# Softmax sums into PSUM and an integer addition moved to VectorE, in an attention and two-MoE kernel on one Trainium2 core

## The chip, the cores and the metric

The kernel runs on one core of a Trainium2 chip. The core has a matrix engine (TensorE, PE in the rows; PEld is its weight load), three engines for elementwise work (VectorE or DVE, ScalarE or ACT, GpSimd or POOL), a queue engine that starts transfers (SyncE, SP), 16 DMA engines, an on-chip memory SBUF and a smaller one, PSUM, of eight banks (2 KB for each of 128 partitions), into which TensorE writes its results. Each engine works through its own instructions in order and waits by semaphores for the others. The metric is the device time of one execution in microseconds (us), lower is better.

## The reference

Three steps on 4608 tokens (batch 8, 576 positions); q, k, v are float32, the weights float64:

```
k_p, v_p = k, v averaged over groups of 8 positions        # (8, 8 heads, 72, 64)
scores = q @ k_p.T / sqrt(64);  scores -= max(scores)
attn = exp(scores);  attn /= sum(attn) + 1e-9;  x = attn @ v_p      # -> (4608, 512)
x = ((x @ w1) * (x @ w2)) @ w3 @ w_out                      # d_ff 1024
h = x @ w_in;  out = (h * sigmoid(1.702 h)) @ w_out2        # d_ff 2048
```

## The kernel before, in words

The weights come as float64, two 32-bit words for each number. `Conv` turns them into float32 on the chip, one 128x512 tile in each `step()`: ScalarE makes a float from the high word (L166) and a small integer from the low one (L168), VectorE shifts the first left by three bits (L169), and GpSimd adds the two as integers (L172), with both inputs and the output in SBUF. A later call splits the result for the matmuls: ScalarE copies the high part (L104), and VectorE or GpSimd, whichever the caller names, subtracts it to get the low part (L105). Every matmul by these parts is done as three (L114 to L116).

Forty conversions come first: 8 tiles of `w_out`, 16 of `w3` (turned by TensorE, L508), 8 of `w1`, 8 of `w2`; they run beside the first attention groups, the product w3 @ w_out and the first block of the first MoE. The other 32, of the second MoE's weights, come in its last two blocks (from about 620 us), where the shift reads PSUM instead of SBUF.

Attention works on 32 groups (one batch element, two heads). A group's steps are spread over "ticks": `g0` transposes k and q (L255, L256, VectorE), `g1` makes the scores in two PSUM banks (L278), takes their maxima (L283) and subtracts them into an SBUF tile (L285), `g2` takes the exponent (L294), `g3` does the rest of the softmax, all on VectorE: row sums (L300), the constant (L301), the reciprocal (L302), the multiplication (L303), then 32x32 transposes (L314). Sums and reciprocals stand in `nm`, a 128x10 tile in SBUF. `g4` splits the result (L368 to L372) and `g6` multiplies by v (L380 to L383) into the same two PSUM banks, and moves the outcome out (L390, L391).

The first MoE works on 9 blocks of 512 tokens; L638 and L641 form the product of its two halves. Blocks 0 to 6 carry the ticks of the remaining groups. The second MoE, from about 770 us, uses nothing that the change touches.

Loads are issued by SyncE in order. The order of the instructions on every queue is settled by the framework, which plans with a cost model of its own (`schedule_with_timeline_sim=True`) when the kernel is built.

Of the kernel before, what the change touches and what calls it, by code (L numbers as in the profile page):

```python
# [12 lines left out]
ALU = mybir.AluOpType  # L13
# [4 lines left out]
P = 128  # L18
T = 512
# [3 lines left out]
def pooled_attention_moe_moe2(  # L23
# [18 lines left out]
    nc = tc.nc  # L42
# [3 lines left out]
    SK = S // POOL  # L46
    DF1 = w1.shape[1]
    DF2 = w_in2.shape[1]
    w1, w2, w3, w_out, w_in2, w_out2 = (w.bitcast(U32) for w in (w1, w2, w3, w_out, w_in2, w_out2))
# [8 lines left out]
    TT = (S + P - 1) // P  # L58
# [36 lines left out]
    def give(*ts):  # L95
        for t in ts:
            if id(t) in held:
                free.append(held.pop(id(t))[1:])
# [19 lines left out]
    def col_tile(w, f):  # L118
        return w[:, 2 * f * P:2 * (f + 1) * P].rearrange("(c p) m -> p c m", p=P)

    def row_tile(w, f):
        return w[f * P:(f + 1) * P, :]

    def sl(i, n=P):
        return slice(i * n, (i + 1) * n)

    class Conv:
# [27 lines left out]
        def step(self):  # L155

            new = None
            if self.staged:
                t, turn, done = self.staged.pop(0)
                lo_w, hi_w = t[:, :, 0], t[:, :, 1]  # L160
                w = cv_p[0].tile([P, T], F32, name="cv", tag="cv", bufs=4)
                wu = w.bitcast(U32)

                e = self.ps[self.n % len(self.ps)] if self.ps else w
                self.n += 1
                nc.scalar.activation(  # L166
                    e, hi_w.bitcast(F32), AF.Prelu, scale=2.0 ** -112, alpha=-2.0 ** 32)
                nc.scalar.activation(lo_w.bitcast(I32), lo_w, AF.Copy, scale=2.0 ** -29)  # L168
                nc.vector.tensor_scalar(  # L169
                    out=wu, in0=e.bitcast(U32), scalar1=3, scalar2=None,  # L170
                    op0=ALU.logical_shift_left)
                nc.gpsimd.tensor_tensor(  # L172
                    out=w.bitcast(I32), in0=w.bitcast(I32), in1=lo_w.bitcast(I32), op=ALU.add)
                give(t)
                new = [w, turn, done]
            mid, old = self.line
            if mid and mid[1]:
                mid[0] = mid[1](mid[0])
            key = old[2](old[0]) if old else None
            self.line = [new, mid]  # L180
            self.load()
            return key
# [4 lines left out]
    conv = Conv()  # L187
# [3 lines left out]
    with pa_ctx:  # L191
# [7 lines left out]
            out=mask[:, 0], in_=mask[:, 0], compare_op=ALU.is_gt, fill=0.0,  # L199
            base=SK, pattern=[[0, D]], channel_multiplier=-1)  # L200
        nc.gpsimd.affine_select(
            out=mask[:, 1], in_=mask[:, 1], compare_op=ALU.is_ge, fill=0.0,
# [8 lines left out]
        for t in s_ts:  # L211
# [6 lines left out]
            out=ident, in_=ident, compare_op=ALU.is_equal, fill=0.0,  # L218
# [6 lines left out]
        g_q, g_k, g_v, g_s = {}, {}, {}, {}  # L225
# [38 lines left out]
        def banks_of(n):  # L264
            return acc[2:] if n < NPE and n % 2 else wk[2:]

        def s_of(n):
            return s_ts[n % 2 if n < NPE else 0]

        def g1(n):  # L270
            sc, s_t = banks_of(n), s_of(n)
            mov = kbd.rearrange("p a s -> p (a s)")
            nm = pa.tile([P, 2 * TT], F32, name="nm", tag="nm", bufs=2)
            g_s[n] = nm
            for half, tts in ((0, range(0, 3)), (1, range(3, TT))):
                w = len(tts) * KW
                for i, tt in enumerate(tts):
                    nc.tensor.matmul(  # L278
                        sc[half][:, i * KW:(i + 1) * KW], qT[:, sl(tt)], mov,
                        start=True, stop=True)  # L280
                ps = sc[half][:, :w].rearrange("p (a s) -> p a s", s=SK)
                m = nm[:, 2 * tts[0]:2 * tts[-1] + 2]
                nc.vector.tensor_reduce(out=m, in_=ps, op=ALU.max, axis=AX.X)  # L283
                na = 2 * len(tts)
                nc.vector.tensor_tensor(  # L285
                    out=s_t[:, tts[0]:tts[-1] + 1, :KW].rearrange("p t (a s) -> p t a s", s=SK),
                    in0=ps.rearrange("p (t a) s -> p t a s", a=2),
                    in1=m.rearrange("p (t a) -> p t a", a=2).unsqueeze(3).to_broadcast(
                        [P, na // 2, 2, SK]),
                    op=ALU.subtract)  # L290
# [3 lines left out]
            nc.scalar.activation(s_t[:, :, :KW], s_t[:, :, :KW], AF.Exp, scale=ESC)  # L294

        def g3(n):
            r, s_t = g_s.pop(n), s_of(n)
            pv = s_t[:, :, :KW].rearrange("p t (a s) -> p t a s", s=SK)
            rv = r.rearrange("p (t a) -> p t a", a=2)
            nc.vector.tensor_reduce(out=rv, in_=pv, op=ALU.add, axis=AX.X)  # L300
            nc.vector.tensor_scalar_add(r, r, 1e-9)  # L301
            nc.vector.reciprocal(out=r, in_=r)  # L302
            nc.vector.tensor_tensor(  # L303
                out=pv, in0=pv, in1=rv.unsqueeze(3).to_broadcast([P, TT, 2, SK]), op=ALU.mult)
            p0 = pa.tile([P, TT, P], F32, name="p0", tag="p0")
            p1 = pa.tile([32, TT, P], F32, name="p1", tag="p1")
            g_s[n] = (p0, p1)
            if n < NPE:
                return
            for r in range(5):  # L310
                for c in range(4):
                    nt = TT if 32 * (c + 1) <= S - (TT - 1) * P else TT - 1
                    dst = p0[32 * r:32 * r + 32] if r < 4 else p1[:32]
                    nc.vector.transpose(  # L314
                        out=dst[:, :nt, 32 * c:32 * c + 32],
                        in_=s_t[32 * c:32 * c + 32, :nt, 32 * r:32 * r + 32])
# [88 lines left out]
        def tick_first():  # L405

            t = tick_n[0]
            tick_n[0] += 1
            for n in range(NPE):
                if t == 2 * n + 6:  # L410
                    g6(n)
            for n in range(NPE):
                s = t - 2 * n
                if s == 0 and n == 0:
                    g0(0)
                elif s == 1:
                    g1(n)
                elif s == 2:
                    g2(n)
                    g0(n + 1)  # L420
                elif s == 3:
                    g3(n)
                elif s == 4:
                    g4(n)
                    g_va(n)
                elif s == 5:
                    g_vb(n)
            if t == 2 * NPE + 4:
                tick_n[0] = 4 * NPE
                give(s_sl)  # L430

        def tick():
            t = tick_n[0]
            if t < 4 * NPE:
                return tick_first()
            tick_n[0] += 1
            n, s = divmod(t, 4)
            if s == 0:
                if NPE <= n - 1 < NG:
                    g4(n - 1)  # L440
            elif s == 1:
                if n < NG:
                    g1(n)
            elif s == 2:
                if NPE <= n - 1 < NG:
                    g6(n - 1)
                if n < NG:
                    g2(n)
                    g_va(n)
                if n + 1 < NG:  # L450
                    g0(n + 1)
            elif n < NG:
                g3(n)
                g_vb(n)

        wo_s, wp_s, w1_s, w2_s = {}, {}, {}, {}
# [87 lines left out]
        def add_3(it, jh):  # L544
            conv.add(w3[sl(it), 2 * jh * T:2 * (jh + 1) * T], w3_turn(it, jh), w3_done(it, jh))

        for jh in range(2):
            for i in range(4):
                j = jh * 4 + i
                conv.add(row_tile(w_out, j), None,  # L550
                         conv.to(wo_s, j, nc.gpsimd if i % 2 else nc.vector, j,
                                 j if j < NA else None))
                if i < 2:
                    add_3(i, jh)
# [3 lines left out]
        for f in range(NF1):  # L558
            conv.add(col_tile(w1, f), None,
                     conv.to(w1_s, f, a=f - FA if 0 <= f - FA < NA else None))  # L560
            conv.add(col_tile(w2, f), None, conv.to(w2_s, f, nc.vector))

        conv.load()
        g_load(0)
# [107 lines left out]
    with tc.tile_pool(name="pb", bufs=1, reuse_waits="tile") as pb, \  # L672
# [238 lines left out]
        for pr in range(1, NPAIR + 1):  # L911
# [100 lines left out]
            m1, U, V, n = [], [], [], 0  # L1012
# [116 lines left out]
```

## Time and profile before

| | |
|---|---|
| median of 3 runs | 1483.03 us (1482.06 to 1484.38) |
| profiled execution: time | 1482.22 us |
| profiled execution: span | 1480.3 us |
| mean granted TensorE clock | 0.993 |
| busy share: TensorE, VectorE, ScalarE, GpSimd | 97%, 67%, 47%, 33% |

The span is the part of the time that the profile covers; 1.9 us lie around it. The shares are means over stages that differ: GpSimd, for one, has most of its work in the first half. A busy TensorE is not TensorE at its peak, since matmuls are pipelined.

### The profile page before, as it was taken

The page shows a single profiled execution, that of the slowest core. Times are in us where ns is not written, and L with a number is a line of the kernel's source. Part 1 is how long each engine was busy: PE and PEld are TensorE (multiplying, and loading weights), DVE is VectorE, ACT ScalarE, POOL GpSimd, SP SyncE. Part 2 cuts the span into 40 slices and gives each one's busy share as a digit, 9 for nine tenths or more (in the row PEclk, how much of TensorE's full clock was granted, in tenths as well). Part 3 has the DMA queues.
Part 4 walks back from the last instruction along what each step waited for, and adds up shares of the span by engine and source line. Part 5 has one row for each costly group of instructions (what it writes and reads, how often), then busy time and mean ns, then how long its engine had stood idle before and what let it go on. Part 6 is the DMA issues. An engine that isn't in the chain of part 4 may idle for free.

```text
span 1480.3 us, 19432 instructions
## 1 busy us (share of the span) xinstructions
PE 1437.6 (97%) x6536; PEld 1186.8 (80%) x6536; DVE 989.9 (67%) x1728; ACT 694.3 (47%) x1212; POOL 491.0 (33%) x589
## 2 busy tenths in 40 slices
PE   5978999999999999999999999999999999999998
PEld 3757888888888888888888887788788888888886
DVE  7889998878787877645536355693559354944554
ACT  6874444434343434366635335552455244634442
POOL 8787865555555555357743200000000000000000
PEclk8999999999999999999999999999999999999999
DMA  9992333323232321089879979867677766785665
GB/s 273 235 232 45 65 77 65 74 49 75 48 75 49 74 44 38 29 288 339 329 232 384 336 237 314 295 200 228 199 237 224 223 199 217 240 237 181 194 213 139
DMA packets 294435, 267.64 MB, mean 181 GB/s; under 512 B 201664, under 2 KB 226240, under 8 KB 294336
## 3 DMA queue, kind: packets, MB, share of 16 engines
q1 hardware_dynamic: 291648, 265.09, 59.8%
q10 hardware_dynamic: 2688, 1.31, 0.3%
q8 instruction: 52, 0.85, 0.2%
q14 instruction: 47, 0.39, 0.1%
HBM read 209.72 MB, written 56.62 MB: 180 GB/s over the span
## 4 chain that ended last, share of the span: by engine, by line
PE 85%; DVE 6%; DMA 4%; ACT 3%; issue 1%; SPq 0%; POOL 0%; DVEq 0%; ACTq 0%; POOLq 0%
PE bk L709 40%; PE wk L114 9%; PE wk L116 8%; PE wk L115 8%; PE acc L116 4%; PE acc L114 4%; PE acc L115 4%; PE wk L278 2%; DMA wud<-wt 2%; PE bk L115 1%; PE bk L116 1%; PE bk L114 1%; DVE s L105 1%; DVE cv L169 1%; DMA st<-wind 1%
## 5 line engine op out<-in xcount | busy, mean ns | idle before, releaser
L709 PE MATMUL bk<-mv,st 128*128 128x512 f32 x1152 | 271.5, 389 | 1.0 <-ACT mv L104 1.0
L709 PE MATMUL bk<-xM,st 128*128 128x512 f32 x1092 | 258.5, 390 | 3.2 <-ACT u L967 1.3
L709 PEld LDWEIGHTS bk<-mv,st 128*128 128x128 f32 x1152 | 216.1, 188 | 46.4 <-ACT mv L104 1.6
L709 PEld LDWEIGHTS bk<-xM,st 128*128 128x128 f32 x1092 | 204.5, 188 | 47.6 <-issue 2.5
L114 PE MATMUL wk<-s,s 128*128 128x512 f32 x576 | 227.9, 397 | 6.2 <-DVE a L641 3.6
L115 PE MATMUL wk<-s,s 128*128 128x512 f32 x576 | 225.4, 392 | 1.6 <-DVE s L391 1.5
L116 PE MATMUL wk<-s,s 128*128 128x512 f32 x576 | 225.3, 392 | 0.1
L314 DVE STREAM_TRANSPOSE p<-s_t 32x160 f32<-32x160 f32 (+1 forms) x560 | 178.5, 319 | 10.5
L115 PE MATMUL acc<-s,s 128*128 128x512 f32 x352 | 140.3, 399 | 1.2 <-POOL s L105 1.1
L116 PE MATMUL acc<-s,s 128*128 128x512 f32 x352 | 139.8, 397 | 1.6 <-DVE s L105 1.6
L114 PE MATMUL acc<-s,s 128*128 128x512 f32 x352 | 132.4, 402 | 7.4 <-DVE s L105 5.0
L114 PEld LDWEIGHTS wk<-s,s 128*128 128x128 f32 x576 | 108.7, 189 | 30.5 <-DVE a L641 4.7
L115 PEld LDWEIGHTS wk<-s,s 128*128 128x128 f32 x576 | 108.5, 188 | 24.0 <-DVE s L391 2.4
L116 PEld LDWEIGHTS wk<-s,s 128*128 128x128 f32 x576 | 108.5, 188 | 23.1 <-DVE s L105 0.5
L105 POOL TENSOR_TENSOR s<-a,s 128x512 fp32r<-128x512 f32 x56 | 73.4, 1310 | 155.1 <-ACT s L104 121.3
L105 DVE TENSOR_TENSOR mv<-g,mv 128x1024 fp32r<-128x1024 f32 x80 | 97.7, 1221 | 33.4 <-ACT mv L104 32.1
L104 ACT CAST mv<-g 128x1024 fp32r<-128x1024 f32 x80 | 84.3, 1053 | 72.5 <-PE bk L709 72.1
L172 POOL TENSOR_TENSOR cv<-cv,s 128x512 int32<-128x512 int32 x72 | 100.7, 1406 | 35.9 <-DVE cv L169 22.7
L114 PEld LDWEIGHTS acc<-s,s 128*128 128x128 f32 x352 | 67.2, 192 | 22.5 <-ACT s L104 4.6
L116 PEld LDWEIGHTS acc<-s,s 128*128 128x128 f32 x352 | 67.2, 191 | 15.7 <-DVE s L105 2.9
L115 PEld LDWEIGHTS acc<-s,s 128*128 128x128 f32 x352 | 67.3, 191 | 14.5 <-POOL s L105 2.3
L638 ACT COPY a<-wk 128x512 f32<-128x512 f32 x72 | 42.0, 583 | 68.4 <-PE wk L116 68.2
(188 smaller groups left out, 2341.8 us busy)
## 6 DMA issues: line engine op xcount, KB each, us to landing
st<-wud SPq DMA_DIRECT2D x96, 512.0 KB, 4.3
st<-wind SPq DMA_DIRECT2D x66, 512.0 KB, 4.7
st<-wind SPq DMA_DIRECT2D x76, 256.0 KB, 4.0
s<-in_moe_w_dram SPq DMA_DIRECT2D x32, 512.0 KB, 6.5
wind<-s SPq DMA_DIRECT2D x32, 512.0 KB, 5.4
s<-in_moe_w_out_dram SPq DMA_DIRECT2D x24, 512.0 KB, 6.6
kr<-in_k_dram SPq DMA_DIRECT2D x128, 72.0 KB, 2.5
qr<-in_q_dram SPq DMA_DIRECT2D x128, 72.0 KB, 2.5
```

Source lines behind the costliest of these rows:

```text
L104: nc.scalar.copy(dst[:, 0], src)
L105: lo_eng.tensor_tensor(out=dst[:, 1], in0=src, in1=f32(dst[:, 0]), op=ALU.subtract)
L114: nc.tensor.matmul(o, a[:, 0, a_sl], b[:, 0, b_sl], start=first, stop=False)
L115: nc.tensor.matmul(o, a[:, 0, a_sl], b[:, 1, b_sl], start=False, stop=False)
L116: nc.tensor.matmul(o, a[:, 1, a_sl], b[:, 0, b_sl], start=False, stop=last)
L169: nc.vector.tensor_scalar(out=wu, in0=e.bitcast(U32), scalar1=3, scalar2=None, op0=ALU.logical_shift_left)
L172: nc.gpsimd.tensor_tensor(out=w.bitcast(I32), in0=w.bitcast(I32), in1=lo_w.bitcast(I32), op=ALU.add)
L278: nc.tensor.matmul(sc[half][:, i * KW:(i + 1) * KW], qT[:, sl(tt)], mov, start=True, stop=True)
L314: nc.vector.transpose(out=dst[:, :nt, 32 * c:32 * c + 32], in_=s_t[32 * c:32 * c + 32, :nt, 32 * r:32 * r + 32])
L638: nc.scalar.copy(a, pa_)
L709: nc.tensor.matmul(o, w[:, x, m], b[:, y], start=first and n == 0, stop=last and n == 2, skip_group_check=True)
```

## The change

Three edits. In `g3` the 128x10 sums and reciprocals no longer stand in `nm` but in the last ten columns of the first of the group's two score banks in PSUM, which `g1` and `g6` leave unused (they take columns 0 to 431 and 0 to 287); the multiplication's two inputs change places, so that the reciprocals are the first. `nm` still takes the maxima. The integer addition L172 goes from GpSimd to VectorE, for all 72 tiles. The subtraction L105 of four of the eight `w_out` tiles and of all `w2` tiles goes from VectorE to GpSimd, so that it is there for all tiles of `w_out`, `w1` and `w2`.

```diff
@@ Conv.step
-                nc.gpsimd.tensor_tensor(
+                nc.vector.tensor_tensor(
                     out=w.bitcast(I32), in0=w.bitcast(I32), in1=lo_w.bitcast(I32), op=ALU.add)
@@ g1
-            g_s[n] = nm
@@ g3
-            r, s_t = g_s.pop(n), s_of(n)
+            s_t = s_of(n)
+            r = banks_of(n)[0][:, T - 2 * TT:]
...
             nc.vector.tensor_reduce(out=rv, in_=pv, op=ALU.add, axis=AX.X)
             nc.vector.tensor_scalar_add(r, r, 1e-9)
             nc.vector.reciprocal(out=r, in_=r)
             nc.vector.tensor_tensor(
-                out=pv, in0=pv, in1=rv.unsqueeze(3).to_broadcast([P, TT, 2, SK]), op=ALU.mult)
+                out=pv, in0=rv.unsqueeze(3).to_broadcast([P, TT, 2, SK]), in1=pv, op=ALU.mult)
@@ the list of conversions
-                         conv.to(wo_s, j, nc.gpsimd if i % 2 else nc.vector, j,
+                         conv.to(wo_s, j, nc.gpsimd, j,
...
-            conv.add(col_tile(w2, f), None, conv.to(w2_s, f, nc.vector))
+            conv.add(col_tile(w2, f), None, conv.to(w2_s, f))
```

## Rows read from the trace of the kernel before

**Rows 1.** Windows: stretch, length, busy (instructions) by engine, PEclk, DMA share, GB/s.

```profile
0.00:180.00 180.00, 148.59 (x686) 116.48 (x687) 152.74 (x262) 119.96 (x250) 144.13 (x171) 0.95 0.73 173
180.00:620.00 440.00, 439.45 (x2115) 370.68 (x2114) 359.75 (x887) 174.81 (x396) 232.44 (x332) 1.00 0.26 57
620.00:770.00 150.00, 149.97 (x664) 123.75 (x663) 74.72 (x108) 81.76 (x146) 90.84 (x72) 1.00 0.81 286
...
20.00:130.00 110.00, 91.25 (x434) 70.33 (x433) 96.27 (x143) 81.70 (x175) 91.13 (x101) 0.92 0.92 213
```

**Rows 2.** Waits of TensorE, 0 to 180 us: total us, times, longest.

```profile
PE wk L508 <- POOL cv L172: 10.6, 2, 9.2
PE acc L114 <- DVE s L105: 5.0, 3, 3.0
PE wk L114 <- DVE a L641: 3.6, 2, 1.9
...
PE acc L115 <- POOL s L105: 1.1, 2, 0.7
```

**Rows 3.** Groups of VectorE by shape, 0 to 180 us: count, busy us, mean ns.

```profile
L169 DVE TENSOR_SCALAR cv<-cv 128x512 uint32<-128x512 uint32 x40 | 30.8, 777 | 10.5 <-ACT cv L166 10.5
L105 DVE TENSOR_TENSOR s<-cv,s 128x512 fp32r<-128x512 f32 x12 | 14.4, 1198 | 1.5 <-ACT s L104 1.5
...
L303 DVE TENSOR_TENSOR s_t<-s_t,nm 128x720 f32<-128x720 f32 x6 | 10.3, 1714 | 0.1
L301 DVE TENSOR_SCALAR nm<-nm 128x10 f32<-128x10 f32 x8 | 9.5, 1182 | 0.1
...
L303 DVE TENSOR_TENSOR s<-s,nm 128x720 f32<-128x720 f32 x2 | 3.4, 1718 | 0.0
```

**Rows 4.** Single lines, whole span: ns min/median/max, first and last start.

```profile
L301 DVE TENSOR_SCALAR nm<-nm x32: 155/173/3399, 30.8 to 610.8; 128x10 f32<-128x10 f32 x32
...
L303 DVE TENSOR_TENSOR s_t<-s_t,nm x30: 895/899/4380, 33.9 to 611.2; 128x720 f32<-128x720 f32 x30
...
L169 DVE TENSOR_SCALAR cv<-wk x32: 675/681/692, 634.0 to 747.1; 128x512 uint32<-128x512 uint32 x32
...
L105 DVE TENSOR_TENSOR s<-wk,s x32: 656/691/693, 11.0 to 767.7; 128x512 fp32r<-128x512 f32 x32
```

**Rows 5.** Groups of GpSimd by shape, 0 to 180 us.

```profile
L172 POOL TENSOR_TENSOR cv<-cv,s 128x512 int32<-128x512 int32 x40 | 54.9, 1377 | 17.3 <-DVE cv L169 4.3 <-DMA s<-in_moe_w_dram 3.5 <-DMA kr<-in_k_dram 1.9
L105 POOL TENSOR_TENSOR s<-cv,s 128x512 fp32r<-128x512 f32 x12 | 15.5, 1295 | 3.0 <-ACT s L104 2.8
```

**Rows 6.** The ending chain within 0 to 155 us, shares by line.

```profile
by line: DVE s L105 9.2%; DVE cv L169 8.9%; DVE p L314 8.0%; DMA s<-in_moe_w_dram 6.6%; issue 6.4%; DVE nm L301 4.8%; DMA qr<-in_q_dram 4.8%; DVE s_t L303 4.5%; ACT cv L166 4.1%; ACT s L104 3.6%; ACT s L168 3.0%; PE wk L114 2.8%; DVE nm L30
```

**Rows 7.** Timeline near 83 us: start, us, instruction [idle before].

```profile
83.51 3.40 DVE L301 TENSOR_SCALAR nm<-nm 128x10 f32<-128x10 f32 x1
...
85.60 1.27 POOL L172 TENSOR_TENSOR cv<-cv,s 128x512 int32<-128x512 int32 x1
```

**Rows 8.** Timeline of the first two conversions.

```profile
5.51 0.43 DVE L169 TENSOR_SCALAR cv<-cv 128x512 uint32<-128x512 uint32 x1 [4.36 <-ACT cv L166]
...
6.66 0.65 ACT L168 ACTIVATE s<-s 128x512 int32<-128x512 uint32 x1
6.78 0.92 DVE L169 TENSOR_SCALAR cv<-cv 128x512 uint32<-128x512 uint32 x1 [0.84 <-ACT cv L166]
...
7.84 1.30 POOL L172 TENSOR_TENSOR cv<-cv,s 128x512 int32<-128x512 int32 x1 [0.42 <-DVE cv L169]
```

**Rows 9.** Timeline of one group's end in the steady state.

```profile
387.62 0.90 DVE L300 TENSOR_REDUCE nm<-s_t 128x10 f32<-128x720 f32 x1 [0.91 <-ACT s_t L294]
...
391.23 0.43 DVE L391 TENSOR_TENSOR s<-wk,s 128x256 fp32r<-128x256 f32 x1
...
399.37 1.42 POOL L372 TENSOR_TENSOR pt<-p,pt 32x576 fp32r<-32x576 f32 x1
...
407.99 0.29 PE L380 MATMUL wk<-ph,vm 128*128 128x288 f32 x1
```

## The prediction, made before any run of the changed kernel

> **What bounds the kernel now.** I read the busy time by stretch first [rows 1]. From 180 us to the end of the first MoE (770) TensorE has work nearly all the time: 439.45 us in 440, then 149.97 in 150. VectorE and GpSimd have room there. What the change does in those stretches is covered by TensorE, as long as no wait gets into TensorE's own queue. The first 180 us are the other kind: TensorE is busy 148.59 us, so 31.4 us are open, VectorE is busy 152.74 and GpSimd 144.13. The case is decided there.
>
> Next, who TensorE waits for in that stretch [rows 2]. The first wait, 9.2 of the 10.6 us put down to L172, is the start, before any weight is converted. Of the rest, VectorE's results (L105, L641) are named for 5.0 and 3.6 us and GpSimd's L105 for 1.1. So VectorE's queue makes TensorE late and GpSimd hardly does, directly.
>
> The row that names the lines of the ending chain within the first 155 us says the same [rows 6]: VectorE's L105, L169 and transposes lead it, and L301 and L303 stand in it with 4.8% and 4.5%, that is 7.4 and 7.0 us.
>
> Last, why L301 costs anything: it adds a constant to 10 columns. Its shortest execution takes 155 ns, the median is 173, but the longest 3399 [rows 4]; in the first 180 us its mean is 1182 over 8, and L303's is about 1.71 us against a median of 899 ns [rows 3, 4]. The timeline shows the long one beside GpSimd's L172 [rows 7]: L301 starts at 83.51 and is done at 86.91, as L172 (85.60, 1.27) ends. Other rows show which VectorE work is never stretched: L105 with one input in PSUM (wk) stays within 656 to 693 ns, and L169 reading wk within 675 to 692, although GpSimd works then too; the same L105 with both inputs in SBUF (cv) has a mean of 1198, and L169 in SBUF of 777 [rows 3, 4]. So an instruction wholly or partly on PSUM escapes GpSimd, and one with all its data in SBUF often waits for it.
>
> The Trainium skill says this as a rule ("SBUF — State Buffer", section "Who interferes with whom"): a VectorE instruction with two SBUF inputs contends with a GpSimd instruction that reads SBUF, and one with at most one SBUF input, outside the two-port modes, does not. The rows agree (1198 against 681 to 691 ns).
>
> **The change part by part.** All terms lie in the first 180 us.
>
> How much of a microsecond of VectorE work reaches the end: from below, the five VectorE entries shown on the chain add up to 35% of it [rows 6]; from above, VectorE is busy 96.27 of 110 us from 20 to 130, 88% [rows 1]. I take one half.
>
> 1. Sums and reciprocals in PSUM. L300, L301 and L302 then write the score bank; L303 has one SBUF input left. Excess today: L301 8 x (1.182 - 0.173) = 8.1 us; L303 10.3 + 3.4 - 8 x 0.90 = 6.5; together 14.6 on VectorE [rows 3, 4]. On the chain itself: 7.4 less four short executions (0.7), and 7.0 less three of 0.90, is 6.7 + 4.3 = 11.0 [rows 4, 6]. From below, half of 14.6 is 7.3. I take 11, since these pieces stand on the chain. What PSUM adds to four small instructions is not shown; L169 needs 0.68 from PSUM and 0.43 in SBUF at 512 columns [rows 4, 8], so at 10 columns next to nothing. Sum: -11.
>
> 2. L172 on VectorE. 32 of its 72 executions lie after 620, under a full TensorE [rows 1]: 0. The other 40 cost 0.68 us each, as L105 with the same 128x512 and no disturbance [rows 4]; no row shows an integer add with a stride on VectorE, so this is the nearest. 40 x 0.68 = 27.2, half is +13.6. Both inputs are in SBUF, so it may wait for GpSimd as L105 (cv) does: from below 0, from above 1.198 - 0.68 = 0.52 each. GpSimd's load in the stretch falls from 144.1 to 144.1 - 54.9 + 15.5 = 104.7 [rows 1, 5], and the most frequent thing to wait for, L172 itself, is gone. I take 0.25: 10 us, half is +5.
>    The same section of the Trainium skill speaks against this part: whichever of the two engines starts first keeps the port for its whole instruction. If each L172 met a whole GpSimd instruction of 1.38 us, that would be 55 us, half 28 in place of 5, and the sum +19. The row of L105 (cv), 0.52, says less.
>
> 3. L105 of four w_out and eight w2 tiles to GpSimd. VectorE loses 12 executions, 14.4 us [rows 3], half is -7.2. GpSimd takes 1295 ns for one [rows 5] against 1198 on VectorE, so the tile itself is ready no earlier; GpSimd has the room that L172 leaves.
>
> 4. L169 keeps its place, but the L172 it ran into is gone. Its excess is 30.8 - 40 x 0.43 = 13.6 us [rows 3, 8]. Between nothing and all of it I take half, 6.8, as GpSimd still has other work; half of that reaches the end: -3.4.
>
> 5. Start. The second conversion's low half is ready at 7.31 (6.66 + 0.65), its shift could be done at 7.21 (6.78 + 0.43). On GpSimd the add ends at 9.14, on VectorE it would at about 8.0 [rows 8]. Nothing else precedes the first matmul: -1.1.
>
> Sum: -11 + 13.6 + 5 - 7.2 - 3.4 - 1.1 = -4.1 us. The profiled execution has a span of 1480.3 us and a time of 1482.22, 1.9 around it; 1482.2 - 4.1 = 1478.1. The runs' median is 0.8 above the profiled one, so the same runs would show about 1479: 0.28% faster. A difference under 0.2% (3 us) can't be told from none here.
>
> The most there is to win is 31.4 - 9.2 = 22 us of open TensorE time. And the transfers are nearly at their limit: the DMA share from 20 to 130 is 0.92 [rows 1], so what VectorE gives back beyond a few microseconds would meet the weight loads as the next to be late.
>
> **The rivals.**
> - Nothing to measure, because the loads set the pace of the first 130 us (share 0.92), or because terms 1 and 2 cancel. For it: -11 and +18.6 are each larger than their sum. Time 1480 to 1486; about 1483.
> - Slower, by the queue of VectorE. If VectorE sets the stretch alone, every term counts in full: 27.2 + 40w - 14.4 - 6.8 - 14.6 - 1.1 = 40w - 9.7, where w is the wait of one L172. It decides at w = 0.24 us. With w = 0.52, as L105 (cv) has today, the sum is +11, 1494; with L169 unrelieved +18, 1501. For it: VectorE is at 88% and the change gives it more instructions than it takes. Against it: GpSimd's load falls by 27%.
> - Slower, by the bank. If the row sums must wait for other users of their PSUM bank, and not only for their own columns, then in the steady state L300 (387.62) has to come after the evacuation of the previous group's output (L391, done at 391.66): 4.0 us later. What hides it: GpSimd's L372 is done at 400.79 and TensorE takes the result at 407.99, 7.2 us later [rows 9]. Should the shift be longer than that in the 24 groups of that stretch, what is beyond stands in TensorE's queue; 0.3 us in each group is 7 us, 1490. The Trainium skill ("PSUM — Partial Sum Buffer", section "PSUM bank collisions raise a hardware error") says that two engines may not use one bank at the same time in the same partitions, so that a wait over the whole bank is likely; by the 7.2 us above it is hidden.
> - The PSUM form doesn't escape GpSimd. Then term 1 is 0 and the sum is +7, 1490. Rows 4 speak against it; small.
>
> The order on each queue comes from a planner whose costs the trace doesn't show. A new order can cost or give some microseconds anywhere in the first 180; this is in the range.
>
> **How the numbers follow.** Forecast, faster by about 4 us: 0.45. No measurable change: 0.25. Slower by VectorE's queue 0.18, by the bank 0.08, PSUM form useless 0.04: 0.30. Low end: no wait at L172 and L169's excess all gone, -11 + 13.6 - 7.2 - 6.8 - 1.1 = -12.5, so 1470. High end: VectorE alone with w = 0.52, +11, so 1494, which takes in the bank's 1490 and leaves out the worst.
>
> **What would show it.** L301 below 0.3 us and L303 near 0.90 in every execution: term 1 right. L172 on VectorE near 0.93 on average over the first 40: term 2; above 1.2 it is the second rival. VectorE busy about 154 us in the first 180 (152.7 + 27.2 + 10 - 14.4 - 6.8 - 14.6), GpSimd about 105, TensorE's open time there down from 31.4 to about 27. From 180 to 770 TensorE without gaps; a gap before L278 or L380 there would be the bank. I would be wrong if the open time before 180 grows although L301 and L303 are short: then the added L172 weighs more than the waits they removed.

## The result and the profile after

The changed kernel takes 1491.4 us (median of 6 runs, 1488.4 to 1494.2) where the kernel before takes 1483.7 beside it (1480.1 to 1485.1): ratio 1.0055, 95% interval 1.0040 to 1.0070. It is slower; the forecast had it 0.28% faster. The profiled execution took 1490.33 us, its span is 1488.6.

Windows of the changed kernel over the stretches of [rows 1], with the same columns:

```profile
0.00:180.00 180.00, 145.36 (x655) 114.63 (x656) 159.58 (x300) 120.16 (x250) 108.29 (x151) 0.92 0.71 175
180.00:620.00 440.00, 440.00 (x2125) 372.59 (x2124) 349.66 (x853) 172.98 (x392) 226.71 (x322) 1.00 0.26 56
620.00:770.00 150.00, 147.40 (x645) 121.37 (x644) 100.59 (x160) 81.50 (x146) 50.38 (x42) 0.99 0.80 286
```

Two stretches lost. In the first 180 us TensorE's open time grew from 31.4 to 34.6 us and its granted clock fell from 0.95 to 0.92. From 620 to 770, where nothing was open, 2.6 us are. From 180 to 620 there is no gap.

VectorE's groups by shape, first 180 us of the changed kernel (beside [rows 3]), then L301 and L303 over its whole span (beside [rows 4]):

```profile
L172 DVE CUSTOM_DVE_ANT_0 cv<-s,cv 128x1024 uint16<-128x1024 uint16 x40 | 33.7, 846 | 1.4
L169 DVE TENSOR_SCALAR cv<-cv 128x512 uint32<-128x512 uint32 x40 | 31.4, 790 | 6.8 <-ACT cv L166 6.6
```

```profile
L301 DVE TENSOR_SCALAR wk<-wk x30: 142/176/177, 30.7 to 621.5; 128x10 f32<-128x10 f32 x30
...
L303 DVE TENSOR_TENSOR s_t<-wk,s_t x30: 889/908/909, 32.6 to 622.0; 128x720 f32<-128x720 f32 x30
```

Nearly every duration came out as the prediction had it: L301 never above 0.18 us, L303 never above 0.91, L172 0.85 (0.93 was expected), VectorE busy 159.6 us (154) and GpSimd 108.3 (105). Only L169 got no relief, 790 ns against 777. And the time still went the other way. So the step that failed is not the price of L172, L301 or L303, but what a microsecond of VectorE is worth, and where.

### The profile page after: what moved, and what is told of

It reads as the page before. It is cut to its first block, busy times and chain, and to the rows that moved or that the text cites. A ratio compares the mean times of both kernels' runs of the same rounds, so it can differ in the third digit from the quotient of the medians.

```text
span 1488.6 us, 19393 instructions
## 1 busy us (share of the span) xinstructions
PE 1441.1 (97%) x6536; PEld 1192.4 (80%) x6536; DVE 1015.3 (68%) x1788; ACT 694.6 (47%) x1212; POOL 409.6 (28%) x529
## 4 chain that ended last, share of the span: by engine, by line
PE 84%; DMA 5%; DVE 4%; ACT 2%; issue 1%; POOL 1%; SPq 1%; DVEq 0%; ACTq 0%; POOLq 0%
PE bk L709 39%; PE wk L114 8%; PE wk L116 8%; PE wk L115 8%; PE acc L115 4%; PE acc L116 4%; PE acc L114 4%; PE wk L277 2%; DMA wud<-wt 2%; DMA s<-in_moe_w_dram 1%; PE bk L115 1%; PE bk L116 1%; PE bk L114 1%; DVE cv L172 1%; DMA st<-wind 1%
## 5 line engine op out<-in xcount | busy, mean ns | idle before, releaser
L709 PE MATMUL bk<-mv,st 128*128 128x512 f32 x1152 | 271.5, 389 | 0.4 <-DMA st<-wud 0.4
L709 PE MATMUL bk<-xM,st 128*128 128x512 f32 x1092 | 258.5, 390 | 2.4 <-DMA st<-wind 1.2
L709 PEld LDWEIGHTS bk<-mv,st 128*128 128x128 f32 x1152 | 216.1, 188 | 45.8 <-issue 1.0
L709 PEld LDWEIGHTS bk<-xM,st 128*128 128x128 f32 x1092 | 204.6, 188 | 46.6 <-issue 1.9
L105 DVE TENSOR_TENSOR mv<-g,mv 128x1024 fp32r<-128x1024 f32 x80 | 97.7, 1222 | 31.9 <-ACT mv L104 30.5
L104 ACT CAST mv<-g 128x1024 fp32r<-128x1024 f32 x80 | 84.3, 1054 | 70.4 <-PE bk L709 69.3
L638 ACT COPY a<-wk 128x512 f32<-128x512 f32 x72 | 42.2, 586 | 132.1 <-PE wk L116 113.1
L105 POOL TENSOR_TENSOR s<-a,s 128x512 fp32r<-128x512 f32 x56 | 73.2, 1308 | 101.8 <-ACT s L104 70.8
L369 POOL TENSOR_TENSOR ph<-p,ph 128x576 fp32r<-128x576 f32 x32 | 45.5, 1421 | 124.3 <-ACT ph L368 124.2
```

What stands on the lines that cost most here:

```text
L104: nc.scalar.copy(dst[:, 0], src)
L105: lo_eng.tensor_tensor(out=dst[:, 1], in0=src, in1=f32(dst[:, 0]), op=ALU.subtract)
L369: nc.gpsimd.tensor_tensor(out=ph[:, 1], in0=s0, in1=f32(ph[:, 0]), op=ALU.subtract)
L638: nc.scalar.copy(a, pa_)
L709: nc.tensor.matmul(o, w[:, x, m], b[:, y], start=first and n == 0, stop=last and n == 2, skip_group_check=True)
```

## Where the second loss is: the last 32 additions

TensorE's waits, 620 to 775 us, changed kernel; then its VectorE timeline there, TensorE's, and windows of 10 us:

```profile
PE wk L114 <- DVE s L105: 2.3, 1, 2.3
PE acc L114 <- ACT s L104: 0.3, 1, 0.3
```

```profile
737.45 2.88 DVE L172 CUSTOM_DVE_ANT_0 cv<-s,cv 128x1024 uint16<-128x1024 uint16 x2
...
746.45 1.76 DVE L172 CUSTOM_DVE_ANT_0 cv<-s,cv 128x1024 uint16<-128x1024 uint16 x1
748.13 0.68 DVE L105 TENSOR_TENSOR s<-wk,s 128x512 fp32r<-128x512 f32 x1
```

```profile
748.87 0.50 PE L114 MATMUL wk<-s,s 128*128 128x512 f32 x1 [2.26 <-DVE s L105]
749.20 0.39 PE L115 MATMUL wk<-s,s 128*128 128x512 f32 x1
749.43 0.40 PE L116 MATMUL wk<-s,s 128*128 128x512 f32 x1
...
750.81 0.63 PE L115 MATMUL wk<-s,s 128*128 128x512 f32 x1
751.23 0.63 PE L116 MATMUL wk<-s,s 128*128 128x512 f32 x1
```

```profile
730.00:740.00 10.00, 10.00 (x46) 8.29 (x45) 9.88 (x12) 7.71 (x14) 7.86 (x6) 1.00 0.79 264
740.00:750.00 10.00, 7.40 (x32) 5.50 (x31) 10.00 (x14) 5.15 (x10) 6.30 (x5) 1.00 0.70 277
750.00:760.00 10.00, 10.00 (x39) 8.06 (x38) 9.30 (x12) 4.65 (x8) 6.21 (x5) 0.83 0.65 225
```

VectorE is full from 730 to 750. L172 stands in front of L105 and lasts 1.76 us, and TensorE waits 2.26 us for that L105. After the gap the clock is granted at the lower of its two levels (1.2 against 2.4 GHz) for some 3 us: one matmul starts every 0.42 us (750.81 to 751.23) where just after the gap it was every 0.23 (749.20 to 749.43). The prediction's "32 of its 72 executions lie after 620, under a full TensorE" was read from a mean over 150 us (VectorE 74.72 busy, half). The kernel before, whose second MoE starts 9 us earlier, in the same two windows:

```profile
730.00:740.00 10.00, 10.00 (x46) 8.29 (x45) 6.65 (x10) 5.93 (x11) 10.00 (x8) 1.00 0.67 265
740.00:750.00 10.00, 10.00 (x46) 8.28 (x45) 7.19 (x9) 4.67 (x9) 10.00 (x9) 1.00 0.86 274
```

VectorE was free for 6.2 of these 20 us. The changed kernel's L172 takes 8.2 us of the 20.

## The experiments

Ratios are to the kernel before, run on the same chip, with 95% intervals. The last column is taken from the timeline of the profiled execution: when TensorE starts the second MoE (its first L709). It leaves out what happens later; the stretch from there to the end varies by several microseconds from profile to profile, with no work of it changed (707.3 to 717.5 us). Each entry is one execution: e1 and e8, whose orders differ by two instructions, lie 2.9 us apart.

| run | what differs from the kernel before | ratio | second MoE starts |
|---|---|---|---|
| before | | 1 | 770.58 |
| e1 | sums in PSUM | 0.9977 (0.9963 to 0.9992) | 765.66 |
| e2 | all 72 additions on VectorE | 1.0091 (1.0077 to 1.0105) | 778.55 |
| e3 | 12 subtractions on GpSimd | 1.0126 (1.0106 to 1.0146) | 785.30 |
| e4 | all three, last 32 additions on GpSimd | 1.0033 (1.0021 to 1.0045) | 775.59 |
| e5 | sums, subtractions | 1.0048 (1.0031 to 1.0065) | 779.15 |
| e6 | sums, first 40 additions | 1.0055 (1.0040 to 1.0071) | 775.35 |
| e7 | sums, last 32 additions | 1.0000 (0.9982 to 1.0017) | 767.76 |
| e8 | sums, first 2 additions | 0.9975 (0.9963 to 0.9988) | 768.54 |
| changed | all three | 1.0055 (1.0040 to 1.0070) | 779.64 |
| e10 | sums; first 40 shifts left out | 0.9975 (0.9951 to 1.0000) | 768.41 |
| e11 | sums, subtractions; shifts left out | 1.0026 (1.0016 to 1.0036) | 773.18 |
| e12 | all three; shifts left out | 1.0043 (1.0027 to 1.0059) | 775.61 |
| e13 | sums; L301 left out | 1.0021 (1.0010 to 1.0032) | 775.16 |
| e14 | sums; L301 twice | 1.0011 (1.0000 to 1.0023) | 771.90 |
| e15 | all three; L301 left out | 1.0080 (1.0064 to 1.0097) | 779.00 |
| e16 | all three; L301 twice | 1.0081 (1.0067 to 1.0095) | 778.47 |
| e17 | L300 in two parts | 1.0052 (1.0036 to 1.0068) | 775.70 |

### The parts alone

The theories at this point. A: the loss comes from L172 on VectorE, in the first stage and in the last 32, and the sums in PSUM gain. B: the sums' bank makes someone wait. C: only the planner's new order, within 5 us either way.

The edits are those of the diff ahead, each by itself; e4 is the whole change but for the last 32 additions:

```diff
@@ e4, Conv.step
-                nc.vector.tensor_tensor(
+                (nc.gpsimd if self.ps else nc.vector).tensor_tensor(
```

> Only the sums and reciprocals go to PSUM. Theory A (the loss comes from L172 on VectorE, the softmax part gives back waits): 4 to 8 us faster than before, 1476 to 1480, L301 under 0.2 us. Theory B (the bank makes other users wait): 3 us or more slower, 1487 or above, with gaps before L278 or L380 between 180 and 620. Theory C (any edit makes a new planned order, and the order alone moves the time): anywhere within 5 us of before.

> Only L172 goes to VectorE, all 72. Theory A: slower than the full change, since the waits of L301 and L303 stay and VectorE keeps the twelve subtractions: 1492 to 1500, with gaps of TensorE before 180 and about 745. Theory B: no slower than before, 1481 to 1486. Theory C: within 5 us of before.

> Only the twelve subtractions go to GpSimd. Theory A: VectorE is relieved by 14 us before 180 while GpSimd, at 144 of 180 us, gets 16 more: 0 to 4 us faster, 1480 to 1484. Theory B: as before, 1484. Theory C: within 5 us of before.

> The full change, but the last 32 integer additions (from 620 us on) stay on GpSimd. Theory A: the 2.6 us of open TensorE time near 745 and the slow matmuls behind it go, so 4 to 5 us less than the full change: 1486 to 1488. A rival A2 (all of the loss arises before 180): as the full change, 1490 to 1492. Theory B: as the full change.

e1 gains, as expected of it, 0.23%. But VectorE's busy time in the first 180 us fell by 5.3 us only (152.74 to 147.46), where L301 and L303 had 14.6 us of excess to lose. The same groups in e1:

```profile
L169 DVE TENSOR_SCALAR cv<-cv 128x512 uint32<-128x512 uint32 x40 | 36.3, 917 | 9.5 <-ACT cv L166 9.0
L105 DVE TENSOR_TENSOR s<-cv,s 128x512 fp32r<-128x512 f32 x12 | 16.1, 1343 | 0.7 <-ACT s L104 0.7
```

L169 went from 777 to 917 ns and L105 (cv) from 1198 to 1343 [rows 3]: 5.5 and 1.7 us of the freed time. In this order part of the wait for GpSimd moved to the instructions that still have all their data in SBUF. From 180 to 620 TensorE is busy 438.85 of 440 us in e1, 0.60 less than before [rows 1]: theory B finds no wait worth the name there.

e2 and e4 came out as theory A had them (1496.9 and 1487.6 us): the additions alone lose 0.91%, and taking the last 32 back to GpSimd wins part of the loss.

e3 was the surprise: moving the subtractions, which had looked like the safest gain, costs 1.26%. Its VectorE timeline near the end of the conversions:

```profile
128.54 7.49 DVE L301 TENSOR_SCALAR nm<-nm 128x10 f32<-128x10 f32 x1
136.07 0.22 DVE L302 RECIPROCAL nm<-nm 128x10 f32<-128x10 f32 x1
136.32 0.91 DVE L303 TENSOR_TENSOR s_t<-s_t,nm 128x720 f32<-128x720 f32 x1
137.33 6.64 DVE L314 STREAM_TRANSPOSE p<-s_t 32x160 f32<-32x160 f32 x20
144.00 0.69 DVE L641 TENSOR_TENSOR a<-wk,a 128x512 f32<-128x512 f32 x1
```

Ten columns take 7.49 us, beside a row of GpSimd instructions without a pause, and TensorE waits 8.9 us for the L641 at the end of this list. L301 is done at 136.03, in the first pause of GpSimd's row (136.00 to 136.08):

```profile
134.72 1.28 POOL L105 TENSOR_TENSOR s<-cv,s 128x512 fp32r<-128x512 f32 x1
136.08 0.31 POOL L342 TENSOR_TENSOR vt<-vtf,vt 32x64 fp32r<-32x64 f32 x1
```

I took that for the cause of e3's loss; e5 was to show it.

### The parts in pairs

> The sums and reciprocals in PSUM and the twelve subtractions on GpSimd; every L172 stays on GpSimd. Theory A (the subtractions alone lost time because L301, with its ten columns in SBUF, was kept waiting 7.5 us by a row of GpSimd instructions): with L301 on PSUM that wait can't occur, L301 stays below 0.3 us, VectorE loses 14 us of its own work in the first 180 us against the softmax part alone, and the time is 1475 to 1482 us, at or below the 1479.2 of the softmax part alone. Rival C (GpSimd's longer queue, 12 x 1.3 us more with all 40 L172, is what lost the time): 1490 us or more, with TensorE waiting for GpSimd's L105 or L172.

> The sums and reciprocals in PSUM and the first 40 integer additions on VectorE; the twelve subtractions stay on VectorE and the last 32 additions on GpSimd. Theory A (VectorE's queue in the first 180 us decides): VectorE is busy about 147 + 40 x 0.85 - 7 = 174 us at most there, 167 at least, more than the 159 of the version with the subtractions moved, and the time is 1488 to 1494 us. Rival C (the moved subtractions cost, not the additions): below 1484 us.

> The sums and reciprocals in PSUM and only the last 32 integer additions on VectorE. Theory A: about 4 us over the softmax part alone, 1482 to 1485 us, with the first 180 us as there (VectorE about 147 us, TensorE about 150.5) and TensorE's gap of 2 to 3 us near 745 us, put down to VectorE's L105. Theory C (a new order of the planner everywhere): the first 180 us differ by over 1 us of TensorE's time, and there is no gap near 745.

> The sums and reciprocals in PSUM and only the first two integer additions on VectorE. If the start's gain reaches the end (as the fifth term of the prediction had it): the first matmul at about 8.0 us instead of 9.1, and 1478 us, 1.1 below the softmax part alone. If a load or VectorE's queue takes it back: first matmul at 8.0 and 1479 to 1480 us.

e5 took that theory down. L301 is short there and VectorE is busy 130.7 us, 17 fewer than in e1, yet the kernel is 0.7% slower than e1. Its longest waits of TensorE between 20 and 60 us, and VectorE's timeline ahead of the first:

```profile
PE wk L351 <- DVE s_t L303: 4.5, 1, 4.5
PE wk L277 <- DVE qT L256: 4.0, 1, 4.0
```

```profile
27.20 2.56 DVE L169 TENSOR_SCALAR cv<-cv 128x512 uint32<-128x512 uint32 x1
...
30.49 1.53 DVE L169 TENSOR_SCALAR cv<-cv 128x512 uint32<-128x512 uint32 x1
...
32.28 1.44 DVE L169 TENSOR_SCALAR cv<-cv 128x512 uint32<-128x512 uint32 x1
33.65 0.89 DVE L303 TENSOR_TENSOR s_t<-wk,s_t 128x720 f32<-128x720 f32 x1
```

Now L169 is the one that waits, ahead of L303. The time is also in the range of e5's rival C (1490.7 us), the longer queue of GpSimd. TensorE's waits put down to GpSimd's L105 in the first 180 us, in e3 and in e5 (1.1 us in e1):

```profile
PE acc L115 <- POOL s L105: 4.1, 3, 1.8
PE acc L115 <- POOL s L105: 3.6, 3, 1.8
```

That is 2.5 to 3.0 us more than in e1, a part of these losses at most.

e6 takes 1491.9 us, in the range of theory A, but VectorE is busy 158.8 us and not 167 to 174: L169 falls to 620 ns there. So the time agrees and the load that was to explain it does not.

e7 gives the price of the last 32 additions a second time. From 119 to 631 us its L638 start within 0.1 us of those of e1. Then the gap comes, again 2.3 us and again put down to L105, and the ratio is 0.0023 above e1's. The pair e4 and the changed kernel gives 0.0022; their L638 starts lie 0.4 us apart from 185 to 641 us. Either is about 3.3 us. The intervals are wide for such a difference, but the gap is in both traces and in neither of the partners. The other versions agree: TensorE waits for VectorE's L105 between 620 and 775 us in all that have the last 32 additions on VectorE (1.6 us in e2, 2.3 in e12, 2.5 in e15, 0.5 in e16, where 1.9 more are put down to L104), and in none that leaves them on GpSimd.

The lower clock does not follow each time. In e7's trace it stays at 1.00 behind the gap, and the second MoE starts 2.1 us after that of e1; in the changed kernel's it fell, and the start is 4.1 us after that of e4:

```profile
730.00:740.00 10.00, 7.41 (x32) 5.50 (x31) 10.00 (x14) 5.41 (x10) 6.31 (x5) 1.00 0.71 281
740.00:750.00 10.00, 10.00 (x46) 8.15 (x45) 9.20 (x13) 4.24 (x8) 6.48 (x5) 1.00 0.63 214
```

e8 shows that a gain at the start does not come through: the first matmul is at 7.96 us instead of 8.81 in e1, with the same order on every queue but for the two additions, and neither the ratio nor the start of the second MoE is better. From 119 us on its L638 start 3.1 us later than those of e1. e7's first matmul, at 9.50 us, is 0.7 us later than e1's, and that is lost as well.

### What VectorE's time is worth

If VectorE's queue sets the pace, then less of it must help, whatever the reason for its load. The first forty shifts were left out of three versions:

```diff
@@ Conv.step
+                if self.ps:
-                nc.vector.tensor_scalar(
-                    out=wu, in0=e.bitcast(U32), scalar1=3, scalar2=None,
-                    op0=ALU.logical_shift_left)
+                    nc.vector.tensor_scalar(
+                        out=wu, in0=e.bitcast(U32), scalar1=3, scalar2=None,
+                        op0=ALU.logical_shift_left)
```

> The sums and reciprocals in PSUM; the first forty shifts L169 are left out (the weights come out wrong). VectorE loses 36 us in the first 180. If VectorE's queue sets the stretch by one half (the factor of the prediction): 18 us faster than the softmax part alone, about 1462 us, no less than 1458 (TensorE's open time there is 29.5 us, 8 of it the start). If the loads set it: 1474 to 1479 us.

> The sums and reciprocals in PSUM, the twelve subtractions on GpSimd, and the first forty shifts L169 left out. Theory A, mended (the subtractions on GpSimd cost 11 us because L169, in SBUF, waits for GpSimd's now unbroken row, and L303 stands behind it): without L169 the difference is gone, within 4 us of the version without shifts that keeps the subtractions on VectorE. Rival C (GpSimd's own queue is late): 8 us or more above that version.

> The changed kernel with the first forty shifts L169 left out. VectorE loses 31 us in the first 180. Theory A (after the change VectorE's queue sets the stretch): 15 us or more faster than the changed kernel, 1476 us or less. Rival (the loads, which lead the changed kernel's chain of waits, set it): 1486 us or more.

VectorE lost 31.7, 35.8 and 25.6 us of busy time in the first 180 us (147.46 to 115.78, 130.69 to 94.86, 159.58 to 133.95). The ratios fell by 0.0002, 0.0022 and 0.0012: 0.3, 3.3 and 1.8 us. That is 0.01 to 0.09 us for one of VectorE, where the prediction took one half. The intervals are as wide as these differences, and by the starts of the second MoE it is -0.09 to 0.17; one half would have been 13 to 18 us. My mended theory for e5 and the theory of VectorE's queue for the changed kernel fall with it: e11 is still 0.5% above e10, and e12, with 13.5 us less work on VectorE than e1, is 0.66% above e1 (0.22 of it the last 32 additions). Rival C's time for e11 (8 us or more above e10) is met by 8.3 us between the medians; but TensorE's waits put down to GpSimd's L105 are 1.8 us there, and its open time is no longer than e10's (29.3 and 30.0 us). What e11 loses by stays open. The line that names the ending chain within the first 155 us, e1 and then e10 (behind L169 the line numbers are one higher in e10):

```profile
by line: DVE cv L169 7.7%; DVE p L314 7.7%; DVE s L105 7.4%; PE acc L114 6.8%; PE acc L115 5.9%; PE acc L116 5.7%; issue 5.4%; DMA s<-in_moe_w_dram 4.4%; DMA qr<-in_q_dram 4.2%; SPq L229 4.1%; DMA kr<-in_k_dram 3.5%; PE wk L114 2.9%; PE wk 
```

```profile
by line: SPq L230 21.6%; DMA s<-in_moe_w_dram 18.6%; DVE s L105 6.7%; PE wk L116 4.3%; PE wk L114 4.2%; DVE p L315 4.1%; issue 3.9%; PE wk L115 3.8%; PE acc L114 3.2%; DMA kr<-in_k_dram 3.0%; PE acc L116 2.8%; PE acc L115 2.8%; SPq L151 2.7
```

Take VectorE's L169 out of the chain, and the loads (SyncE's issues and the weights' transfers) stand there with 40%. Two chains of nearly the same length side by side would look like this, and the one that the profile names is only the one that ended last. No run changes the loads, so that they set the pace is not shown.

### The same work in another order

What was left was the order of the queues, which the planner makes anew with each edit. L301 is 0.17 us of work and changes nothing in the result (it adds 1e-9 to a sum of at least 1). To leave it out or to do it twice gives the versions other orders for next to no work: in the traces, TensorE's instructions in e13 and e14 differ in their order from those of e1 by about as much as those of the changed kernel do.

```diff
@@ g3, e13 and e15
-            nc.vector.tensor_scalar_add(r, r, 1e-9)
@@ g3, e14 and e16
-            nc.vector.tensor_scalar_add(r, r, 1e-9)
+            nc.vector.tensor_scalar_add(r, r, 1e-9); nc.vector.tensor_scalar_add(r, r, 1e-9)
@@ g3, e17 (kernel before)
-            nc.vector.tensor_reduce(out=rv, in_=pv, op=ALU.add, axis=AX.X)
+            nc.vector.tensor_reduce(out=rv[:, :3], in_=pv[:, :3], op=ALU.add, axis=AX.X)
+            nc.vector.tensor_reduce(out=rv[:, 3:], in_=pv[:, 3:], op=ALU.add, axis=AX.X)
```

> The sums and reciprocals in PSUM, and L301 (0.17 us on ten columns, 32 times, 5 us of VectorE's 988) left out: it adds 1e-9 to a sum that is at least 1. The work is the same, but the planner makes another order, as far from that of the softmax part alone as the changed kernel's is. Theory D (the engines that do the work decide): 1477 to 1483 us, as the softmax part alone. Theory O (the order decides): anywhere in 1475 to 1492, and of the four runs of this kind at least one softmax version is above 1486 or one changed kernel below 1484.

> The sums and reciprocals in PSUM, and L301 done twice. Theory D: 1478 to 1484 us. Theory O: anywhere in 1475 to 1492.

> The changed kernel with L301 left out. Theory D: 1488 to 1494 us, as the changed kernel. Theory O: anywhere in 1475 to 1495.

> The changed kernel with L301 done twice. Theory D: 1489 to 1495 us. Theory O: anywhere in 1475 to 1495.

> The kernel before, with L300's sums taken in two instructions (three and two of its five tiles), about 0.1 us of VectorE more for each of 32 groups: the same work in another order. Theory D (the engines decide, and the sums in PSUM gain 0.2%): 1482 to 1486 us. Theory O (the order of the queues decides, the sums in PSUM are worth nothing measurable): anywhere in 1477 to 1492, so that the kernel before and the version with the sums in PSUM cover the same span.

Windows of the first 180 us: e1, e13, e14, then e17.

```profile
0.00:180.00 180.00, 150.54 (x708) 119.64 (x709) 147.46 (x265) 121.28 (x253) 146.54 (x179) 0.96 0.71 175
```

```profile
0.00:180.00 180.00, 142.30 (x654) 112.60 (x655) 138.44 (x251) 119.73 (x250) 141.84 (x173) 0.91 0.71 173
```

```profile
0.00:180.00 180.00, 150.62 (x679) 119.60 (x680) 145.41 (x277) 121.15 (x252) 145.10 (x180) 0.92 0.72 175
```

```profile
0.00:180.00 180.00, 148.16 (x660) 116.46 (x661) 150.95 (x274) 120.28 (x249) 144.45 (x172) 0.92 0.72 173
```

The order is worth as much as the change. The sums in PSUM run from 0.23% faster to 0.21% slower in three orders. The kernel before is 0.52% slower in its second order, nearly what the whole change cost (0.55%). The changed kernel's three orders lie closer together, 0.55 to 0.81% slower, and all above the worst of the sums in PSUM. So neither theory holds alone. Theory D's ranges were passed by 3.3 us in e13, 0.3 in e14, 1.8 in e15 and 5.5 in e17, and kept in e16. Theory O's own test (one softmax version above 1486) was met by 0.3 us, one changed kernel below 1484 did not come, and e15 is 0.8 us above O's range.

VectorE's load doesn't follow the time here either. In e13 VectorE is busy 138.4 us, 14.3 fewer than in the kernel before (1.4 of them are the L301 left out), with L169 at 786 ns. That is about the 14.6 of term 1, and e13 is 3.1 us slower than the kernel before.

The versions differ by the clock as well as by the gaps. In the first 180 us TensorE is busy 150.5 us at a mean granted clock of 0.96 in e1 and 145.4 us at 0.92 in the changed kernel: by the product, an estimate, 144.5 against 133.7 us at full clock. Of these 10.8 us, 5.2 are open time and 5.6 the lower clock. Where only the order differs, it can be the clock alone. e17 has the open time of the kernel before (31.8 and 31.4 us), but a clock of 0.92 and not 0.95: 136.3 against 141.2 us, 4.9 less, and its second MoE starts 5.1 us later. e14 has that of e1 (29.4 and 29.5 us) at 0.92 and not 0.96: 5.9 us less, and the second MoE starts 6.2 us later. So the sum of the open time doesn't tell the loss. What in an order brings the clock down is not shown.

### The price of the shared access by itself

> A kernel that leaves out all of the computation (its output is zeros) and measures one cost: GpSimd does 1, 3 or 6 integer additions of 128x512 without a pause while VectorE, after one instruction on PSUM alone, does one of six instructions. Theory A (an SBUF-only VectorE instruction is kept waiting until a row of GpSimd instructions has a pause): ten columns in SBUF, the shift and the integer addition take 2 to 3 us longer with each two further additions (longest about 7 us beside six of them); the ten columns in PSUM and the multiplication with one input in PSUM keep 0.2 and 0.7 us. Rival (only one GpSimd instruction is waited for): never more than 1.3 us on top, whether 1, 3 or 6 stand in the row.

> Leaves out all of the computation (the output is zeros): 0, 1, 3 or 6 independent integer additions of 128x512 on GpSimd without a pause, and about 1 us after their start one VectorE instruction of six kinds. Row theory: with all data in SBUF it lasts 1 us or less over its time alone beside one addition, about 3 us beside three and 5 to 7 us beside six; on PSUM it keeps its time. One-instruction theory: at most 1.3 us over its time alone in every case.

e9 told little: the additions of its row used one result after the other, and the planner let small copies into the row. e18 has independent additions and a start that touches PSUM only:

```diff
@@ e18, for k = 0, 1, 3, 6 and each of the six instructions
+            for i in range(k):
+                nc.gpsimd.tensor_tensor(out=a[i], in0=a[i], in1=b, op=ALU.add)
+            nc.vector.tensor_scalar_add(ps, go, 1.0)
+            form()
```

Its VectorE timeline: ten columns in SBUF beside none, one and six additions, then the shift, the integer addition and the multiplication with one input in PSUM, each beside none and six:

```profile
20.77 0.17 DVE L58 TENSOR_SCALAR c<-c 128x10 f32<-128x10 f32 x1 [0.31 <-ACT pr L86]
...
22.50 0.47 DVE L58 TENSOR_SCALAR c<-c 128x10 f32<-128x10 f32 x1 [0.23 <-ACT c L85]
...
29.01 0.47 DVE L58 TENSOR_SCALAR c<-c 128x10 f32<-128x10 f32 x1 [0.23 <-ACT c L85]
...
52.60 0.43 DVE L64 TENSOR_SCALAR c<-c 128x512 uint32<-128x512 uint32 x1 [0.23 <-ACT c L85]
...
61.53 0.72 DVE L64 TENSOR_SCALAR c<-c 128x512 uint32<-128x512 uint32 x1 [0.23 <-ACT c L85]
...
87.75 0.69 DVE L72 CUSTOM_DVE_ANT_0 c<-c,d 128x1024 uint16<-128x1024 uint16 x1 [0.23 <-ACT c L85]
...
97.48 0.98 DVE L72 CUSTOM_DVE_ANT_0 c<-c,d 128x1024 uint16<-128x1024 uint16 x1 [0.23 <-ACT c L85]
...
105.89 0.69 DVE L76 TENSOR_TENSOR c<-pr,c 128x512 f32<-128x512 f32 x1 [0.30 <-ACT pr L86]
...
115.01 0.69 DVE L76 TENSOR_TENSOR c<-pr,c 128x512 f32<-128x512 f32 x1 [0.30 <-ACT pr L86]
```

With all its data in SBUF an instruction waits 0.3 us here, about the rest of the addition that is running, and no longer beside six than beside one. With one input in PSUM it does not wait. The one-instruction theory holds in this setting. The Trainium skill says the same ("SBUF — State Buffer", section "Who interferes with whom"): whoever starts first has the shared access for its whole instruction. The traces of the kernel itself go beyond that: 3.40 us [rows 7] and 7.49 us (e3) for ten columns span several GpSimd instructions, and e18 doesn't reproduce it. The kernel's rows mix instructions of several lines and shapes, those of e18 are all alike; what else is needed for such a wait stays open.

## Why the prediction was wrong, step by step

- **What bounds the first stage.** That TensorE waits for VectorE's results was read rightly [rows 2, 6]. That VectorE's load sets them was not: 26 to 36 us less of it bring 0.3 to 3.3 us (e10 to e12). The factor of one half on terms 2 to 4, and the 11 of 14.6 in term 1, are the step that failed. Its bounds (35% and 88%) measured how much VectorE stood on one chain, not how close the next chain was. The sentence on the loads, "the next to be late", was there, but only as a cap at a few microseconds, and that it is the loads is not shown. The prediction's own sign of being wrong came: the open time grew, from 31.4 to 34.6 us, though L301 and L303 are short. Its reading, that the added L172 weighs more than the waits removed, is not borne out: in e12, with 25.6 us less on VectorE, the open time is still 33.2.
- **Term 1, -11.** The durations fell as costed. In e1 the 14.6 us became 5.3, as L169 and L105 took over 7.2 us of waiting, while in e13 nearly all of it came off VectorE. The time moved by -3.4 us in e1 and by +3.1 and +1.6 in e13 and e14: nothing that can be told from the order.
- **Term 2, first forty, +18.6.** L172's price was right (0.85 us, of it 0.17 waiting). If a microsecond added weighs what one taken away did (0.09 at most by the ratios, 0.17 by the starts of the second MoE), its 33.7 us are worth 3 to 6 us. With two chains of nearly the same length added work can weigh more than work taken away; no run tests that. In e6 they cost 11.6 on top of e1, the order's share included; the runs do not separate the two.
- **Term 2, last 32, 0.** This term, put at nothing from a mean over 150 us, measured 3.3 us, in two pairs with the gap in view. It is the only part of the loss that is pinned down.
- **Term 3, -7.2.** Not found. In the one order tried of each, the subtractions on GpSimd cost 18.7 us alone (e3), cost 10.5 on top of e1 (e5) and gain 3.3 on top of e6 (e4). These differences hold the order's share, up to 7.7 us by e17. As long as L172 is on GpSimd, the move costs in all three pairs (7.6 in e11 over e10); with L172 gone, in e4, it does not. That is the pattern of rival C, GpSimd's own queue, of which the traces show 2.5 to 3.0 us. The rest is open.
- **Term 4, -3.4.** L169 got no shorter: with L172 on VectorE and more L105 on GpSimd it still met GpSimd. Where the subtractions stay on VectorE (e6) it takes 620 ns, 24.6 us in all, the half of its excess that this term took. So terms 3 and 4 were not independent.
- **Term 5, -1.1.** The first matmul came 1.2 us earlier (9.2 to 8.0 of waiting); e8 shows it lost again before the second MoE.
- **The order.** It "can cost or give some microseconds" was in the range and not in the sum. Its spread, 0.52% or 7.7 us between two orders of the kernel before, is more than the whole sum (-4.1).
- **The rivals.** The sign is that of "slower, by the queue of VectorE", and its sum fits too: with w = 0.17 and L169 unrelieved, 40w - 9.7 + 6.8 is +3.9. Its mechanism is what e12 speaks against: 25.6 us less on VectorE gave 1.8. So the fit of that number is luck. "By the bank" is out (no gaps from 180 to 620), and so is "PSUM doesn't escape" (L301 0.18, L303 0.91 at most).

Of the 8.2 us that the change costs, 3.3 are the last 32 additions. The other 4.9 (e4's 0.33%) lie inside what another order of the kernel before does by itself. All three orders of the changed kernel are above all three of the sums in PSUM, by 0.34% or more, and the last 32 additions are 0.22 of that; so a little of it may belong to the engines. How much, and by which wait, stays open: with two or three orders of each version the runs do not part it.

e1, the sums in PSUM alone, beats both kernels, in the order that it got. Its two siblings, e13 and e14, beat the changed kernel only.

## What to carry to other kernels

Before a saving on an engine is counted at some factor, take all of that engine's work of one kind away and time it: here three such runs showed that a microsecond saved on VectorE was worth far less than one half, whatever the waits were named. (What a microsecond added costs, they do not show.) A stage's mean hides its last tens of microseconds; price added work in the window where it lands, and look at the granted clock as well as at the gaps. Where a planner makes the order, time each version in two or three orders of the same work, or 0.5% can't be told from luck.

## What the runs showed of the hardware that was not expected

- An int32 addition of two tensors on VectorE runs as a custom instruction on 128x1024 uint16 and takes 0.69 us for 128x512, as long as a float subtraction (0.69, e18); on GpSimd it is 1.26.
- Beside GpSimd, a VectorE instruction of ten columns costs GpSimd nothing, an addition or a subtraction costs it 0.45 us: in e18 the row of three takes 3.69 us beside the one and 4.14 beside the others.

```profile
23.95 3.69 POOL L82 TENSOR_TENSOR a<-a,b 128x512 int32<-128x512 int32 x3 [1.01 <-ACT b L80]
...
91.96 4.14 POOL L82 TENSOR_TENSOR a<-a,b 128x512 int32<-128x512 int32 x3 [1.53 <-ACT b L80]
```

- A gap of 2.3 us was followed by some 3 us at the lower clock in the changed kernel (a matmul every 0.42 us instead of 0.23) and by none in e7.
- Two orders of nearly the same work (e17 and the kernel before) had the same open time in the first 180 us (31.8 and 31.4 us) and granted clocks of 0.92 and 0.95.
